# Decode attention on one core: GpSimd hands VectorE its first credits, and ends only after the last wide value matmuls

## The chip, the cores and the metric

One core of a Trainium2 chip. The metric is the device time of one execution in microseconds (us). Every run whose state the record gives is fast, with a mean granted clock of 0.799 to 0.818. "Span" is the time from the first to the last instruction of the program in the profile; the metric is 1.7 to 1.8 us longer than the span in most profiled executions.

A few words on names. The kernel programs the engines by hand. In its code an engine waits for a semaphore to reach a number, or takes (waits and subtracts); another engine or a load adds. A "credit" is such an addition given ahead of time, so that the first pass through a loop does not wait for something that has not happened yet. PE is the TensorE, DVE the VectorE, ACT the ScalarE, POOL the GpSimd, SP the SyncE.

## The reference

Attention for one query token: 32 query heads, 8 key/value heads, 65,536 keys, head size 128, bfloat16.

```python
B, Hq, Hkv, Sq, Sk, D = 1, 32, 8, 1, 65536, 128
k = jnp.repeat(k, Hq // Hkv, axis=1); v = jnp.repeat(v, Hq // Hkv, axis=1)
scores = jnp.einsum("bhqd,bhkd->bhqk", q, k) * D ** -0.5
return jnp.einsum("bhqk,bhkd->bhqd", softmax(scores, axis=-1), v)
```

Keys and values together are 268 MB, each byte used once. The arithmetic per byte is small.

## The kernel before

There are eight groups (one key/value head each), and each has two key blocks and two value blocks of 128 x 256 rows. SyncE issues all loads; VectorE transposes keys and weights; TensorE makes scores and the weighted sum of values; ScalarE does the exponential; GpSimd only clears buffers, copies 16 columns of the query per group, and gives credits. These are the parts that matter here (cuts marked `# ...`):

```python
# SyncE
load_k(0, 0)
load_k(0, 1)
sp.sem_inc(s_vd, 2)                 # VectorE's two credits for its value weights
for g in range(1, G):
    for b in range(2):
        load_k(g, b)                # waits for score matmuls (s_sc)
        load_v(g - 1, b)            # waits for value matmuls (s_vc), then gives s_vd
# ...
# GpSimd, start
GP.mark(gp.memset(wz[:, :, :], 0.0))
gp.memset(zs[:, :], 0.0).then_inc(s_cl, 1)    # credit: the sum buffer is clear
n = GP.mark(gp.memset(ident[:, :], 0.0))
# ... identity matrix
gp.sem_inc(s_v[1], 16 * (2 * G - 3))
gp.sem_inc(s_v[2], 16)
# ...
# VectorE, one group (loop)
y_sum()                             # takes s_cl
transposes(0, 0, SL)                # keys, first block
# ...
transposes(1, 0, 128)
d_take(s_vd)
weights(1)                          # writes the buffer that the value matmuls read
transposes(1, 128, SL)
# ...
# GpSimd, end
GP.wait((s_sc, 16 * G))
gp.sem_inc(s_sd, 1)
GP.wait((s_dv, d_sum(G)))
gp.sem_inc(s_w, 4)
```

The last value block is loaded in eight pieces. The first three (records 101 to 103 in the trace's own numbering) feed the "wide" matmuls; the last five are small and feed 32 small matmuls, then ScalarE scales the result and stores 1 KB.

Of the kernel before, what the change touches and what calls it, by code (L numbers as in the profile page):

```python
# [19 lines left out]
G = 8  # L20
# [29 lines left out]
def kernel(  # L50
# [15 lines left out]
    def sb(name, shape, dt):  # L66
        return ctx.enter_context(nc.sbuf_tensor(name, shape, dt))
# [4 lines left out]
    def sem(name):  # L72
        return ctx.enter_context(nc.semaphore(name))
# [17 lines left out]
    zs = sb("zs", [P, 1024 + 4 * D + D + 2], fp32)  # L91
# [21 lines left out]
    s_sc, s_pe, s_vb, s_vc = sem("s_sc"), sem("s_pe"), sem("s_vb"), sem("s_vc")  # L113

    s_sd, s_vd, s_pt, s_ex, s_ds = sem("s_sd"), sem("s_vd"), sem("s_pt"), sem("s_ex"), sem("s_ds")
    s_cl, s_ga = sem("s_cl"), sem("s_ga")
# [11 lines left out]
    sp, act, dve, gp, pe = nc.sync, nc.scalar, nc.vector, nc.gpsimd, nc.tensor  # L128
# [3 lines left out]
    GP = Queue(nc, gp, s_gp)  # L132
# [16 lines left out]
    def load_k(g, b):  # L149
        SP.wait((s_sc, 16 * g - 8 + 8 * b if g else 0))  # L150
        cuts = k_lo + [SL] if (g, b) in ((0, 0), (G - 1, 1)) else [0, 128, SL] if g == 0 else [0, SL]
        for lo, hi in zip(cuts, cuts[1:]):
            load(k, g, b, 1 + b, s_k[b, lo], lo, hi)
# [23 lines left out]

    load_k(0, 0)
    load_k(0, 1)

    sp.sem_inc(s_vd, 2)
    for g in range(1, G):
        for b in range(2):
            load_k(g, b)
# [5 lines left out]
    act.dma_start(out=q_in[:, :], in_=q[0, :, 0, :]).then_inc(s_q, 16)  # L190

    GP.mark(gp.memset(wz[:, :, :], 0.0))
    gp.memset(zs[:, :], 0.0).then_inc(s_cl, 1)
    n = GP.mark(gp.memset(ident[:, :], 0.0))
    GP.after(n)
    p_ident = GP.mark(gp.affine_select(
        out=ident[:, :], in_=ident[:, :], compare_op=ALU.not_equal, fill=1.0, base=0,
        pattern=[[-1, P]], channel_multiplier=1,
    ))

    gp.sem_inc(s_v[1], 16 * (2 * G - 3))

# [22 lines left out]
    def d_sum(g):  # L225
        return d_qT + 4 * g + 1
# [296 lines left out]
    gp.sem_inc(s_sd, 1)  # L523
    GP.wait((s_dv, d_sum(G)))
    gp.sem_inc(s_w, 4)


# [28 lines left out]
```

## Time and profile before

| | before |
|---|---|
| time, median of the first 3 runs | 629.46 us (629.42 to 630.25) |
| span of the profiled run | 627.8 us |
| load queue, share of the 16 DMA engines' span | 99.1% |
| moved | 268.45 MB at 428 GB/s |
| PE / DVE / ACT / POOL busy | 56% / 55% / 5% / 1% |

First, the page of the kernel before: busy time with its share of the span and number of instructions, then the DMA queues with packets, MB, and share.

```profile
span 627.8 us, 7062 instructions
PE 354.6 (56%) x2142; PEld 139.1 (22%) x2142; DVE 345.5 (55%) x154; ACT 34.4 (5%) x26; POOL 8.8 (1%) x40
...
q1 hardware_dynamic: 6944, 268.45, 99.1%
q8 instruction: 1, 0.02, 0.0%
q10 hardware_dynamic: 56, 0.01, 0.0%
q14 instruction: 1, 0.01, 0.0%
```

No engine is near 100% except the DMA engines (99.1%): the kernel is bound by its loads. The two queues that the profile marks `instruction` and not as data (q8 and q14): each holds one packet within the span, of 16,384 and 8,192 bytes.

The table of windows of the kernel before: window, length, busy us of each engine with counts, granted TensorE clock, DMA share, GB/s.

```profile
core 0: us, PE busy (x) PEld busy (x) DVE busy (x) ACT busy (x) POOL busy (x), PEclk, DMA share, GB/s
40.00:80.00 40.00, 24.40 (x93) 9.49 (x92) 30.76 (x15) 3.94 (x3) 0.77 (x4) 0.80 1.00 433
...
610.00:622.00 12.00, 7.24 (x61) 2.15 (x62) 0.60 (x1) 0.00 (x0) 0.00 (x0) 0.59 0.98 407
622.00:628.00 6.00, 2.48 (x40) 2.01 (x34) 1.47 (x4) 0.36 (x1) 0.00 (x0) 0.97 0.20 67
```

Loads fill everything but the last few us (DMA share 0.98 from 610 to 622 us, 0.20 after). What the last few us hold is shown by the end of the chain of waits (start, length, what):

```profile
608.60 12.41 DMA io<-in_v_dram
621.00 0.04 issue
621.05 1.02 PE acc L253 x5
622.07 0.02 PE pb L347
622.10 1.84 PE pf L358 x28
623.94 0.32 PE pf L247 x2
624.26 0.24 PE pf L358 x4
...
624.59 0.36 ACT o L486
```

The store that follows is issued at 624.98 us and lands at 626.36 us; then comes a closing barrier to 627.8 us. GpSimd leads that barrier: the last of the others comes at 626.74 us, GpSimd's wait is at 626.77, its release at 627.21, and the waits of the four others follow at 627.25 to 627.26 us. Its instructions there, by the view of the program's closing line (count, shortest/median/longest ns, first and last start):

```profile
L551 POOLq EVENT_SEMAPHORE  x4: 17/17/17, 626.8 to 627.7; - x4
L551 POOLq DRAIN  x3: 34/34/112, 612.0 to 627.5; - x3
```

The four semaphore instructions are wait, release, wait, release. The trace has them at 626.77, 627.21, 627.62 and 627.70 us: 0.44 us from the first wait to its release, but 0.08 us for the second pair.

### The profile page before, as it was taken

The page shows a single profiled execution, that of the slowest core. Times are in us where ns is not written, and L with a number is a line of the kernel's source. Part 1 is how long each engine was busy: PE and PEld are TensorE (multiplying, and loading weights), DVE is VectorE, ACT ScalarE, POOL GpSimd, SP SyncE. Part 2 cuts the span into 40 slices and gives each one's busy share as a digit, 9 for nine tenths or more (in the row PEclk, how much of TensorE's full clock was granted, in tenths as well). Part 3 has the DMA queues.
Part 4 walks back from the last instruction along what each step waited for, and adds up shares of the span by engine and source line. Part 5 has one row for each costly group of instructions (what it writes and reads, how often), then busy time and mean ns, then how long its engine had stood idle before and what let it go on. Part 6 is the DMA issues. An engine that isn't in the chain of part 4 may idle for free. (4 is left out here: it accounts for less than half of the span.)

```text
span 627.8 us, 7062 instructions
## 1 busy us (share of the span) xinstructions
PE 354.6 (56%) x2142; PEld 139.1 (22%) x2142; DVE 345.5 (55%) x154; ACT 34.4 (5%) x26; POOL 8.8 (1%) x40
## 2 busy tenths in 40 slices
PE   1865483827638275481844808458183571886346
PEld 0322131312213032130321303123031230332112
DVE  7795835649066490754807557084670946684210
ACT  0000100020000200002000020000200002000100
POOL 2000000000000000000000000000000000000000
PEclk9979596977959679596785968859588695899676
DMA  8999999999999999999999999999999999999996
GB/s 366 436 468 401 468 401 468 401 468 401 468 401 468 401 468 401 468 401 459 409 455 413 443 426 434 434 422 447 413 455 409 459 401 468 401 434 434 434 434 269
DMA packets 7002, 268.48 MB, mean 428 GB/s; under 512 B 856, under 2 KB 1112, under 8 KB 1496
## 3 DMA queue, kind: packets, MB, share of 16 engines
q1 hardware_dynamic: 6944, 268.45, 99.1%
q8 instruction: 1, 0.02, 0.0%
q10 hardware_dynamic: 56, 0.01, 0.0%
q14 instruction: 1, 0.01, 0.0%
HBM read 268.44 MB, written 0.01 MB: 428 GB/s over the span
## 5 line engine op out<-in xcount | busy, mean ns | idle before, releaser
L300 PE MATMUL acc<-io,wz 128*128 x1024 | 271.0, 417 | 187.2 <-PEq L121 157.5
L372 DVE STREAM_TRANSPOSE io<-io 128x4096 uint32<-128x4096 uint32 x64 | 279.9, 4416 | 157.9 <-DVEq L121 157.9
L300 PEld LDWEIGHTS acc<-io,wz 128*128 x1024 | 105.8, 103 | 352.4 <-issue 273.6
L253 PE MATMUL acc<-io,et 128*16 128x512 bf16 x1016 | 72.4, 416 | 19.3 <-PEq L121 19.2
L439 ACT ACTIVATE zs<-acc,nmb 128x2048 bf16<-128x2048 f32 x8 | 15.7, 1967 | 556.5 <-DVE nmb L419 556.5
L409 DVE TENSOR_REDUCE mg<-acc 128x1 f32<-128x2048 f32 x8 | 18.3, 2292 | 48.2 <-DVEq L121 48.2
L253 PEld LDWEIGHTS acc<-io,et 128*16 128x16 bf16 x1016 | 27.6, 94 | 58.5 <-issue 35.6
L247 PE MATMUL pf<-zs,sel 128*4 128x130 f32 (+1 forms) x20 | 5.7, 387 | 53.3 <-PEq L121 53.3
L375 DVE STREAM_TRANSPOSE et<-zs 128x1024 bf16<-128x1024 bf16 x17 | 20.8, 1226 | 22.7 <-SPq L158 12.8
L449 ACT ACTIVATE acc<-wz 128x2560 f32<-128x2560 bf16 (+2 forms) x8 | 16.3, 2040 | 1.0 <-ACT zs L439 0.2
L411 DVE TENSOR_REDUCE m<-pt 1x4 f32<-1x128 f32 x8 | 2.2, 279 | 22.6 <-DVEq L121 22.6
L518 POOL COPY wz<-qT 32x16 bf16<-32x16 bf16 x32 | 6.1, 192 | 513.3 <-PE acc L300 441.1
L325 PE MATMUL pt<-et 128*16 128x512 bf16 x32 | 13.1, 411 | 0.0
L247 PEld LDWEIGHTS pf<-zs,sel 128*4 128x4 f32 x20 | 1.1, 83 | 53.9 <-issue 53.7
L383 DVE TENSOR_REDUCE zs<-zs 128x128 f32<-128x512 f32 x9 | 6.1, 681 | 7.6 <-DVEq L121 7.6
L422 DVE TENSOR_TENSOR zs<-acc,sely 128x512 f32<-128x512 f32 x8 | 8.5, 1064 | 0.0
L471 DVE TENSOR_TENSOR zs<-acc,sely 128x512 f32<-128x512 f32 x1 | 0.7, 691 | 11.5 <-PE acc L253 11.5
L342 PE MATMUL pb<-ident,nrow 1*128 1x1 f32 x8 | 1.5, 189 | 7.5 <-PEq L121 7.5
L325 PEld LDWEIGHTS pt<-et 128*16 128x16 bf16 x32 | 3.1, 97 | 4.5 <-issue 1.4
L340 PE MATMUL pt<-ident,mg 128*1 128x128 f32 x8 | 2.2, 270 | 2.6 <-PEq L121 2.6
L419 DVE COPY nmb<-pb 128x1 f32<-128x1 f32 x8 | 1.3, 159 | 3.9 <-DVEq L121 3.9
L204 DVE MEMSET acc<- 128x2560 f32 x1 | 2.2, 2192 | 1.6 <-SPq L64 1.6
(29 smaller groups left out, 20.6 us busy)
## 6 DMA issues: line engine op xcount, KB each, us to landing
io<-in_v_dram SPq DMA_DIRECT2D x5, 4096.0 KB, 17.0
io<-in_k_dram SPq DMA_DIRECT2D x8, 2048.0 KB, 27.3
io<-in_k_dram SPq DMA_DIRECT2D x2, 4096.0 KB, 34.2
io<-in_v_dram SPq DMA_DIRECT2D x1, 2048.0 KB, 10.3
io<-in_v_dram SPq DMA_DIRECT2D x1, 1024.0 KB, 12.4
io<-in_v_dram SPq DMA_DIRECT2D x3, 256.0 KB, 12.8
io<-in_v_dram SPq DMA_DIRECT2D x2, 128.0 KB, 12.9
io<-in_k_dram SPq DMA_DIRECT2D x13, 48.4
```

Source lines behind the costliest of these rows:

```text
L247: return pe.matmul(out=pf[0:H, 0:w], lhsT=sel[:, :], rhs=vs[:, 0:w], skip_group_check=True, **kw)
L253: return pe.matmul(out=vacc[32 * c:32 * c + 16, :, :], lhsT=et[:, ch // 2, w0:w0 + 16], rhs=io[:, PS * ch + 4 * tt:PS * ch + 4 * tt + 4, : ...
L300: i = pe.matmul(out=bass.AP(acc, r_o, [[2560, P], [1, 512]]), lhsT=bass.AP(wz, r_w + ((2 * s + e) * WB - 4 * u), [[4 * WB, P], [1, P]]), r ...
L325: pe.matmul(out=pt[0:16, :], lhsT=et[:, 0, 0:16], rhs=et[:, 0, :], start=True, stop=True)
L372: dve.transpose(out=part, in_=part).then_inc(s_kt, 2)
L375: dve.transpose(out=et[:, :, :].rearrange("p i n -> p (i n)"), in_=ex[:, 2 * b:2 * b + 2, :].rearrange("p i n -> p (i n)"),).then_inc(s_et, 1)
L383: DV.mark(dve.tensor_reduce(out=vs[:, 0:D], in_=vy[:, :, :], axis=AX.X, op=ALU.add))
L409: dve.tensor_reduce(out=mg[:, :], in_=sc, axis=AX.X, op=ALU.max).then_inc(s_mg, 1)
L422: dve.tensor_tensor(out=vy[:, :, :].rearrange("p d y -> p y d"), in0=vacc, in1=sely[:, :, None].to_broadcast([P, 4, D]), op=ALU.mult,).the ...
L439: act.activation(out=ex[:, :, :].rearrange("p b n -> p (b n)"), in_=sc, func=ACT.Exp, bias=nmb[:, :], scale=SCALE, accum_out=vs[:, D + g % ...
L449: act.activation(out=part, in_=wz[:, 0, 0:1].to_broadcast([P, part.shape[1]]), func=ACT.Copy).then_inc(s_cl, 1)
L518: gp.tensor_copy(out=wz[r, :, c0:c0 + H].rearrange("p (s w) h -> p s w h", s=2), in_=qTb[r, :, :, g, :],).then_inc(s_w, 1)
```

## The change

The stated intent: GpSimd shall end only after the last wide value matmuls, and shall give VectorE its first credits in SyncE's place. It has three instructions more; SyncE one less.

```diff
     load_k(0, 0)
     load_k(0, 1)
-
-    sp.sem_inc(s_vd, 2)
     for g in range(1, G):
@@
     GP.mark(gp.memset(wz[:, :, :], 0.0))
-    gp.memset(zs[:, :], 0.0).then_inc(s_cl, 1)
+    GP.mark(gp.memset(zs[:, :], 0.0))
     n = GP.mark(gp.memset(ident[:, :], 0.0))
@@
+    gp.sem_inc(s_vd, 2)
+    gp.sem_inc(s_cl, 1)
 
     gp.sem_inc(s_v[1], 16 * (2 * G - 3))
@@
     GP.wait((s_dv, d_sum(G)))
     gp.sem_inc(s_w, 4)
+    GP.wait((s_vb, 2 * G))
```

## The prediction

> **What bounds the kernel.** The loads. The table of DMA queues gives the load queue 99.1% of the 16 engines' span: 268.45 MB at 428 GB/s in 627.8 us. No compute engine is near that (PE 56%, DVE 55%, POOL 1%; first part of the page). In the table of windows the DMA share is 0.97 to 1.02 in every stretch from 40 to 610 us. Only the ends are not load time: the first load is issued at 0.96 us; after the last value bytes (about 623.8 us) come the last small matmuls (to 624.5), the scaling on ScalarE (0.36 us), the 1 KB store (issued 624.98, landed about 626.4) and the closing barrier (to 627.8).
>
> **What the change does, with costs.**
> 1. SyncE loses one semaphore instruction (17 ns in the records) at 4.07 us, behind the six first key loads. It then waits tens of us for score matmuls before its next load. Worth: 0.
> 2. GpSimd gives VectorE's two credits instead, and the clearing credit becomes an instruction of its own, no longer tied to the end of the 1.49 us clearing of the zeros tile. Both fall at about 3.4 us, beside the identity's last step (3.40 us, 0.29 us); the two increments already there are recorded at 3.36 and 3.44 us, so two more are an estimated 0.1 us. VectorE takes the clearing credit near 4.8 us, but its sum starts at 5.56 us behind four transposes, and it then waits until 8.4 us for keys anyway. The other credit is first taken at about 41 us. GpSimd's next copy has 1.9 us of slack. Worth: 0.
> 3. GpSimd's last wait. Before, GpSimd's last useful step is at 594.24 us, SyncE holds it until 611.9 us, and it sits in the closing barrier until 626.77. Now it leaves at about 622.1 us, still 4.5 us ahead of the store's landing that the barrier waits for. Worth: 0 on the chain of waits.
> 4. Side effect: instruction fetch. [...] one 16,384-byte packet on an instruction queue at 623.23 us, taking 1.09 us, right as the loads end. If it is GpSimd's, it can move by some us; before the last value bytes it could delay one DMA engine by up to 1.1 us. And between GpSimd's wait and its release in the closing barrier lie 0.44 us at 626.77, against 0.08 us at the two other such places; if that is a fetch, three more instructions may move it out of the chain (-0.36 us), or not.
>
> **Sum.** 0 on the load stream, -0.4 to +1.1 us at the end, most likely near 0. Runs of the kernel before already spread from 629.42 to 630.25.
>
> Predicted 629.4 us; 8 in 10 between 628.5 and 630.4. Chances: faster by over 2% 0.01, within 2% 0.98, slower by over 2% 0.01.
>
> **What would show it.** Load queue again 99%, about 428 GB/s; first key transpose at about 8.4 us; first value weights at about 41.5 us; GpSimd's final drain at about 622.1 us instead of 612.0; the last chain (value load, small matmuls, scaling, store) the same within 0.3 us. The 16 KiB packet's time and the 0.44 us pause tell step 4.
>
> **What would make it wrong.** A hidden dependence on when GpSimd idles or fetches (a fetch that stalls a DMA engine for longer than its packet's 1.1 us), credits later than VectorE needs them, so that the first group's order shifts and later loads with it[...].

The sum came to -0.4 us (0.44 less 0.08 us) to +1.1 us (the 1.09 us of the one packet on q8), both estimates from the trace of the kernel before.

## The result

Ratios here are the mean time of one kernel's fast runs over that of the other's of the same rounds, so not quite the ratio of the medians quoted.

The changed kernel takes 629.38 us (median of 6 runs, 629.05 to 629.69), the kernel before 629.44 us (median of 6, 629.27 to 630.25). The ratio is 0.9997, 95% interval 0.9984 to 1.001: the same. A second comparison of five rounds (below) gave 0.9994, 0.998 to 1.0007. The timings alone do not resolve a gain.

The profile after, in the same order as before:

```profile
span 627.3 us, 7064 instructions
PE 354.5 (57%) x2142; PEld 139.3 (22%) x2142; DVE 345.5 (55%) x154; ACT 34.4 (5%) x26; POOL 8.8 (1%) x40
...
q1 hardware_dynamic: 6944, 268.45, 99.2%
q8 instruction: 1, 0.02, 0.0%
q10 hardware_dynamic: 56, 0.01, 0.0%
q14 instruction: 2, 0.02, 0.0%
```

The loads are as before. One line differs: queue 14 has two instruction packets within the span instead of one. The trace has the extra one, 8,192 bytes, at 623.53 us, taking 0.31 us; in the kernel before one of the same size came at 627.90 us, just after the span.

The end of the chain of waits after the change:

```profile
608.69 12.42 DMA io<-in_v_dram
621.11 0.04 issue
621.15 1.02 PE acc L254 x5
622.17 0.02 PE pb L348
622.20 1.90 PE pf L359 x28
624.09 0.22 PE pf L248 x2
624.31 0.24 PE pf L359 x4
...
624.64 0.36 ACT o L487
```

Up to ScalarE's last step the two kernels agree within 0.15 us at each piece (624.59 and 624.64 us at the end). The span is 0.45 us shorter nevertheless, so the difference lies behind it, in the closing barrier:

```profile
L553 POOLq EVENT_SEMAPHORE  x4: 17/17/17, 626.7 to 627.2; - x4
L553 POOLq DRAIN  x3: 34/34/64, 622.8 to 627.1; - x3
```

GpSimd's first wait is at 626.73 us (626.77 before), its release at 626.81 us (627.21 before): the pause went from 0.44 to 0.08 us, and that 0.36 us is most of the 0.45 (0.04 us lie before the first wait, and the longest drain behind the release is 0.05 us shorter, 64 ns after 112). It did not vanish, it moved: GpSimd's new last wait is at 622.23 us, and the next instruction, a drain, only at 622.65 us, 0.42 us later (0.14 us for the same pair in e1_wait_only below), where nobody waits for GpSimd.

The credits did nothing to the start. VectorE's first instructions on keys and its first value weights, from the timelines of the kernel before and of the kernel after:

```profile
8.39 4.45 DVE L372 STREAM_TRANSPOSE io<-io 128x4096 uint32<-128x4096 uint32 x1 [2.15 <-DVEq L121]
...
41.50 1.20 DVE L375 STREAM_TRANSPOSE et<-zs 128x1024 bf16<-128x1024 bf16 x1
```

```profile
8.40 4.45 DVE L373 STREAM_TRANSPOSE io<-io 128x4096 uint32<-128x4096 uint32 x1 [2.17 <-DVEq L121]
...
41.50 1.20 DVE L376 STREAM_TRANSPOSE et<-zs 128x1024 bf16<-128x1024 bf16 x1
```

### The profile page after: what moved, and what is told of

It is laid out like the page before. It is cut to its first block, busy times and chain, and to the rows that moved or that the text cites. A ratio compares the mean times of both kernels' runs of the same rounds, so it can differ in the third digit from the quotient of the medians.

```text
span 627.3 us, 7064 instructions
## 1 busy us (share of the span) xinstructions
PE 354.5 (57%) x2142; PEld 139.3 (22%) x2142; DVE 345.5 (55%) x154; ACT 34.4 (5%) x26; POOL 8.8 (1%) x40
## 3 DMA queue, kind: packets, MB, share of 16 engines
q1 hardware_dynamic: 6944, 268.45, 99.2%
```

## The experiments

Two theories of the pause. **Leave-time**: the pause is what GpSimd pays for having sat in the barrier from 612 us on; leaving at 622 us cures it. **Instruction-place**: the pause lies at one fixed place in GpSimd's stream of instructions, and a packet that the profile marks as instructions goes with it (after the change, 8,192 bytes at 623.53 us, 1.3 us behind GpSimd's last wait). Where that place falls is a matter of counting instructions. Below, this place is called the crossing and the packet GpSimd's fetch; what GpSimd does at the place was not shown. A third, **chance**, says that it comes and goes. The twelve runs below all gave correct results, and all had five rounds.

### e1_wait_only: the last wait alone (one instruction more)

```diff
     gp.sem_inc(s_w, 4)
+    GP.wait((s_vb, 2 * G))
```

> Only the last wait of the change (GpSimd also waits for the last wide value matmuls); the credits stay as before. All theories: time within 0.2% of before, because the load queue (99% of the span) is untouched. The pause of 0.44 us between GpSimd's wait and its release in the closing barrier tells them apart. Leave-time theory: the pause is a price for having sat in the closing barrier since 612 us, so it falls to about 0.08 us and the span by about 0.36 us. Instruction-place theory: [...] this adds one of the change's three, so it need not fall. Chance theory: it comes and goes in any kernel.

Measured: 629.05 us (628.80 to 629.33), ratio 0.9991 (0.9977 to 1.0004). Pause 0.085 us; GpSimd's packet at 623.81 us. Span 627.48 us. Both theories are still possible, as the kernel leaves later and has another instruction.

### e2_credits_only: the credits alone (two instructions more)

The diff of the change without its last line.

> Only the credits' move to GpSimd (two more instructions there, one less on SyncE), without the last wait. All theories: time within 0.2% of before; first key transpose on VectorE at 8.4 us, first value weights at 41.5 us. Leave-time theory: GpSimd's last drain is at 612 us again and the pause stays at 0.44 us. Instruction-place theory: the pause may fall to 0.08 us, as GpSimd's later instructions stand two places further on.

Measured: 630.22 us (629.35 to 630.35), ratio 1.0003 (0.999 to 1.0017). GpSimd stops at 612 us as before, yet the pause is 0.083 us: the leave-time theory is in trouble. GpSimd's two drains, 0.10 us apart before, are 0.47 us apart here (611.94 and 612.40 us): the pause is there now. And the packet is fetched at 616.07 us, in the middle of the last value loads. The landing records of those loads show what that does. Record 103 has 16 reports, read here as one from each of the 16 DMA engines; the last three reports of record 101 (the load in flight before the fetch) and of 103 (after it) are, in us:

| | 101, last three | 103, last three |
|---|---|---|
| before | 613.58, 613.58, 613.62 | 620.98, 620.98, 621.00 |
| e2_credits_only | 613.60, 613.61, 613.70 | 621.00, 621.11, 621.53 |

One engine falls 0.42 us behind the next, in a load for which the wide matmuls wait. This was not expected.

There is a second thing in this trace. Its chain of waits has 2.74 us for the 28 small matmuls that took 1.84 us before:

```profile
622.62 2.74 PE pf L359 x28
```

The windows of this kernel around it (the clock is the third figure from the right):

```profile
618.10:621.50 3.40, 1.24 (x17) 0.44 (x17) 0.00 (x0) 0.00 (x0) 0.00 (x0) 1.00 0.99 398
621.50:624.90 3.40, 3.33 (x34) 2.75 (x35) 1.47 (x4) 0.00 (x0) 0.00 (x0) 0.50 0.52 177
624.90:628.40 3.50, 0.90 (x13) 0.67 (x11) 0.00 (x0) 0.36 (x1) 0.00 (x0) 0.99 0.01 3
```

The granted clock was 0.50 for exactly the 3.4 us in which the small matmuls ran, so they took 0.9 us longer. In the other 13 traces the clock was full from 622.7 us at the latest. The clock records of the kernels before and after have stretches at 0.5 or 1.0 of 3.41, 6.83, 10.24 us and so on; what sets them was not shown. Two of the five executions of this kernel had spans of 627.6 and 627.7 us. So this 0.9 us belongs to the execution, not to the credits.

### e3_pad3: three idle instructions more, nothing else

```diff
+    for _ in range(3):
+        gp.sem_inc(s_pad, 1)        # a semaphore that nobody reads
     gp.sem_inc(s_v[1], 16 * (2 * G - 3))
```

> The kernel before with three increments of an unused semaphore on GpSimd at the place where the change puts its credits: nothing but three instructions more. Time within 0.2% of before. Leave-time theory: pause 0.44 us, last drain at 612 us. Instruction-place theory: pause 0.08 us, span 0.36 us shorter, as after the change, which also adds three.

Measured: 630.34 us (629.35 to 630.74), ratio 1.0013 (0.9999 to 1.0026). Pause 0.079 us with the last drain at 612 us: the instruction-place theory's figure. But the span of the profiled run is 627.61 us, not 0.36 us shorter: the packet comes at 598.47 us, and the slowest DMA engine is 0.58 us behind the next in record 103. What the pause gave back, the lag took: the last store went out at 625.37 us, 0.40 to 0.54 us later than in the two traces of the kernel before.

### e4_before_again: the kernel before as a null run

> The kernel before, unchanged, as a null run: ratio 1.000 within 0.1%. Its trace shows whether the 0.44 us pause and the span of 627.8 us repeat. Leave-time and instruction-place theories: pause 0.44 us again. Chance theory: the pause may be 0.08 us.

Measured: 629.39 us (629.24 to 629.58), ratio 0.9998 (0.9984 to 1.0011). Pause 0.440 us again; lag 0.03 us. Chance is now unlikely, and the fourteen traces together leave it no room. The span was 627.45 us against 627.80 us in the first trace of the same kernel, so one span is no measure of 0.36 us (0.21 us of this difference is the last store's own time, 1.17 against 1.38 us); the pause and the lag, read as differences inside one trace, are.

### e5_pad1: one idle instruction more

The edit of e3_pad3 with a range of 1.

> The kernel before with one increment of an unused semaphore more on GpSimd at the start, no last wait. Instruction-place theory (the first four experiments gave it): [...] it pauses for about 0.36 us and soon after an 8,192-byte instruction packet is fetched. One instruction more puts the crossing between GpSimd's drain at 612.0 us and its wait in the closing barrier. So: pause in the closing barrier 0.08 us; an 8,192-byte packet at about 616 us; the last DMA engine's share of the final value loads 0.4 to 0.55 us behind the next one's, last value bytes at about 624.2 us instead of 623.8. Net on the span about +0.05 us (+0.4 lag, -0.36 pause), if the clock in the tail is full. Leave-time theory: GpSimd leaves at 612 us as before, so pause 0.44 us, no packet before 624 us, no lag.

Measured: 629.49 us (629.40 to 631.07), ratio 1.0006 (0.9992 to 1.002). Pause 0.086 us, packet at 615.91 us, lag 0.37 us, span 627.66 us, last value bytes at 624.04 us. The place was foretold from counting alone. The leave-time theory falls here: this kernel leaves GpSimd idle from 612 us as before and does not pause.

### e6_pad20: twenty idle instructions more

> Twenty increments more instead of one. Instruction-place theory: the crossing falls behind the last copy for the fourth group, at about 291 us, and the packet is fetched at about 295 us, in the middle of the load stream. If a lag of one DMA engine is kept until the end, the slowest engine is 0.4 to 0.55 us behind the next in the last value loads, as with a fetch at 598 us; if it is made up in 320 us of loading, the gap is below 0.1 us as in the kernel before and the span about 0.36 us shorter than before. Time within 0.2% of before either way.

Measured: 629.37 us (629.25 to 629.53), ratio 0.9997 (0.9984 to 1.0011). Pause 0.078 us; lag 0.46 us at the end. In this trace the last report of each earlier load was at most 0.04 us behind the one before it up to 274.6 us, and 0.48 us in the next load, at 294.4 us: an engine that fell behind in mid-kernel did not catch up in the 340 us of loading that were left. The packet came at 283.63 us and not at 295 as expected. Why it came 7 us before the copy at 290.8 us, behind which it was expected, was not shown.

### e7_six_fewer: six instructions fewer

Six semaphore increments of GpSimd are given by ScalarE instead (two after its first load, two after the scores of the first key block, two after those of the second).

> Six semaphore increments of GpSimd are moved to ScalarE (credits that are first needed much later), no last wait, so GpSimd leaves at 612 us. Instruction-place theory: the crossing falls six instructions later, just behind the last one of the span: pause 0.08 us, no 8,192-byte packet of GpSimd's before 627 us, no lag of a DMA engine (gap below 0.1 us), span about 0.36 us shorter than before: 627.1 to 627.5 us, time about 629.1 us at full clock in the tail. Leave-time theory: pause 0.44 us, span as before.

Measured: 629.72 us (629.32 to 629.77), ratio 1.0001 (0.9987 to 1.0014). Pause 0.079 us, no packet of GpSimd's before 627 us, lag 0.08 us, span 627.49 us: all as expected, but the time was to be 629.1 us and is 629.72. This is the one profiled run in which time minus span is not 1.7 to 1.8 us: it is 2.23 us. It is no single look: the five executions of this kernel have 2.17 to 2.23 us, and the 88 executions of the other kernels and of the kernel before whose spans were recorded with the experiments have 1.68 to 1.88 us. So a pause's worth has left the span, not the time: it seems to lie in the 2.17 to 2.23 us that the metric has beyond the span (the pause is not itself in the trace).

### e8_two_fetches: two crossings within the loads

131 idle increments on GpSimd after its copies for the second group.

> 131 increments of an unused semaphore on GpSimd after its copies for the second group, where it idles (67 to 125 us). [...] GpSimd crosses twice within the loads: among these increments at about 70 us, and, 128 instructions on, behind its step at 594.5 us as with three increments. Instruction-place theory: two 8,192-byte packets, at about 70 to 75 us and at about 598 us; if both fall on the same DMA engine, its lag doubles to about 0.8 to 1.1 us in the last value loads and the span grows by about 0.5 us more; if on two engines, two engines lag by 0.4 to 0.55 us and the span is as with one fetch. Leave-time theory: no lag, pause 0.44 us.

Measured: 629.97 us (629.88 to 630.24), ratio 1.0007 (0.9994 to 1.0021). The page of this kernel shows three packets on queue 14:

```profile
span 628.1 us, 7193 instructions
...
q14 instruction: 3, 0.02, 0.0%
```

They are at 73.09, 599.02 and 625.56 us (the last is another engine's: every trace has one near the last store). Inside the row of idle increments, otherwise 0.08 us apart, there is one step of 0.43 us, at 69.45 us. Counted over GpSimd's recorded instructions, the step at 594.5 us, behind which the second crossing was expected, is the 128th after this one (before the run, 128 was an assumption). After two fetches one DMA engine alone is 1.00 us behind the next in record 103 (622.10 against 621.10 us). The loads of this trace show it in two steps: at most 0.03 us up to 61.8 us, 0.31 to 0.36 us from 81.5 to 594.6 us, 0.92 to 1.02 us from 605.0 us on. This is the dose-response: no fetch in the loads 0.02 to 0.09 us, one 0.32 to 0.58, two 1.00.

### e9_wait_same_count: the last wait, at an unchanged count

```diff
     gp.sem_inc(s_v[1], 16 * (2 * G - 3))
-    gp.sem_inc(s_v[2], 16)          # given by ScalarE instead
@@
     gp.sem_inc(s_w, 4)
+    GP.wait((s_vb, 2 * G))
```

> The change's last wait alone, but with one increment of GpSimd's moved to ScalarE, so that GpSimd has as many instructions as in the kernel before. GpSimd leaves at about 622.2 us. Instruction-place theory: the crossing stays where it was before, between GpSimd's wait and its release in the closing barrier: pause 0.44 us, no 8,192-byte packet of GpSimd's before 627 us, span 627.5 to 627.8 us. Leave-time theory: pause 0.08 us, as with the wait alone.

Measured: 629.47 us (629.44 to 629.88), ratio 0.9995 (0.9981 to 1.0009). GpSimd leaves at 622.1 us, and the pause is 0.439 us:

```profile
L551 POOLq EVENT_SEMAPHORE  x4: 17/17/17, 626.7 to 627.6; - x4
L551 POOLq DRAIN  x3: 34/34/112, 622.2 to 627.4; - x3
```

With e5_pad1 this completes the square: late leaving without another instruction leaves the pause, another instruction without late leaving removes it.

### e10_after_again: the change again

> The change as it is, five times beside the kernel before on one chip. Instruction-place theory: pause 0.08 us, the packet at about 623.5 us, gap of the slowest DMA engine in the last wide value load below 0.1 us; where the granted clock in the last 3 us is full, span about 627.1 to 627.5 us, 0.3 to 0.4 us below the kernel before with the same clock; ratio 0.999 to 1.000.

Measured: 629.17 us (629.00 to 630.13), ratio 0.9994 (0.998 to 1.0007). Pause 0.078 us, packet at 623.25 us, lag 0.04 us in record 103, span 627.32 us. Only the very last small load (record 108) has an engine 0.28 us late.

### e11_late_credit: credits that are really late

```diff
-    sp.sem_inc(s_vd, 2)
@@
                 for t in k_lo[1::2]:
                     gp.sem_inc(s_k[0, t], 16 * (2 * G - 2))
+                GP.wait((s_sc, 12))
+                gp.sem_inc(s_vd, 2)
```

(and one other increment moved to ScalarE, to keep the count).

> The two credits of VectorE are given by GpSimd only after the score matmuls of the first half of the second key block (about 43 us), the number of GpSimd's instructions unchanged. This is a real lateness, against none in the change: first value weights at 43 to 44 us instead of 41.5, the next key transpose 1.5 to 2.5 us later. Load-bound theory: the loads in flight cover it, so the time is within 0.1% of before and the last value load is issued within 0.5 us of 608.2 us. Rival (credits are on the critical path): the time grows by 1.5 to 2.5 us.

Measured: 632.93 us (632.21 to 633.20), ratio 1.0047 (1.0033 to 1.006): slower by about 3 us, more than either theory said (it is under 2%, but the interval excludes no change). The credit came at 47.8 us, not at 43, so VectorE stood still for 6.50 us, as its timeline shows:

```profile
47.98 1.25 DVE L372 STREAM_TRANSPOSE et<-zs 128x1024 bf16<-128x1024 bf16 x1 [6.50 <-DVEq L121]
```

SyncE's next key load went out at 63.65 us instead of 57.23, and the value load of 94.89 us at 101.36. By then the queue had run low. The windows of 96 to 104 us, in the kernel before and in this one:

```profile
96.00:104.00 8.00, 0.00 (x0) 0.00 (x0) 3.44 (x1) 0.00 (x0) 0.00 (x0) 0.76 0.91 393
```

```profile
96.00:104.00 8.00, 5.22 (x72) 2.06 (x70) 3.54 (x1) 0.00 (x0) 0.00 (x0) 1.00 0.69 262
```

From the load of 167.78 us (171.09 here) every load up to the first piece of the last value block is 3.2 to 3.7 us late, and the pieces after it 2.8 us. Of 6.45 us of lateness about 3.1 us were covered by the loads in flight (6.45 less 3.3; an estimate). So the load-bound theory as I put it was wrong: the first group's credits do reach the load stream. In the change they are given at about 3.4 us and used at 41.5 us, which is why they cost nothing.

### e12_wait_last: GpSimd waits for the very last matmul

```diff
-    GP.wait((s_vb, 2 * G))
+    GP.wait((s_pe, 1))
```

(on the changed kernel).

> As after the change, but GpSimd waits for the very last matmul instead of the last wide one, so its crossing, pause and fetch fall at about 624.5 to 625.5 us, behind all value loads and before the store's landing. Instruction-place theory: pause in the closing barrier 0.08 us, packet at about 625.2 us, span equal to that after the change or up to 0.1 us shorter (the packet at 623.5 us still met the last bytes). If the packet meets the store's descriptors instead, the span could be up to 0.3 us longer.

Measured: 629.61 us (629.49 to 630.60), ratio 1.0001 (0.9987 to 1.0015). Pause 0.079 us, but the last store took 1.75 us from issue to landing, 1.16 to 1.49 us in the other traces, and the span was 627.76 us. GpSimd's packet is one of two, at 624.57 and 625.57 us, one of which falls within the store's flight. In the other traces the other engine's packet starts between 0.72 us before and 0.02 us after the store's issue (624.98 us here), so the one at 625.57 us is GpSimd's. It ended at 625.94 us, 0.95 us after the issue, and the store's last 256-byte packet started just then, against 0.81 to 0.82 us after the issue elsewhere. So the fetch seems to have held up the store, and the order of all fourteen stores (below) supports it; no run was made to test this. Later is not better than the change's place.

### All traces together

Lag is the last report of record 103 less the one before it. "Fetch" is GpSimd's own packet, told by its moving with the crossing.

| kernel | GpSimd's instructions | leaves at us | pause us | fetch at us | lag us | span us |
|---|---|---|---|---|---|---|
| before / again | 0 | 612 | 0.44 / 0.44 | 627.9 / 627.7 | 0.02 / 0.03 | 627.80 / 627.45 |
| e9_wait_same_count | 0 | 622 | 0.44 | 628.0 | 0.09 | 627.69 |
| e5_pad1 | +1 | 612 | 0.09 | 615.9 | 0.37 | 627.66 |
| e2_credits_only | +2 | 612 | 0.08 | 616.1 | 0.42 | 628.50 (half clock) |
| e3_pad3 | +3 | 612 | 0.08 | 598.5 | 0.58 | 627.61 |
| e6_pad20 | +20 | 612 | 0.08 | 283.6 | 0.46 | 627.60 |
| e8_two_fetches | +131 | 613 | 0.08 | 73.1, 599.0 | 1.00 | 628.14 |
| e7_six_fewer | -6 | 612 | 0.08 (time minus span is longer by about 0.45) | behind the span | 0.08 | 627.49 |
| e11_late_credit | 0 | 615 | 0.44 | 631.0 | 0.03 | 630.94 |
| e12_wait_last | +3 | 625 | 0.08 | 625.6 | 0.06 | 627.76 |
| e1_wait_only | +1 | 622 | 0.09 | 623.8 | 0.03 | 627.48 |
| the change / again | +3 | 622 | 0.08 / 0.08 | 623.5 / 623.2 | 0.07 / 0.04 | 627.35 / 627.32 |

A count confirms the instruction-place theory: in each trace in which the pause can be seen, it lies between GpSimd's 68th and 69th recorded instruction, wherever that falls (the barrier in before, e4, e9 and e11; the new last wait in the change and e12; the drains in e2; the idle increments in e8). Where that place is at 612.0 us or earlier, in the full load stream, GpSimd's packet starts 3.6 to 4.5 us behind it (e6 aside, where the packet came before the step behind which it was expected); where it is at 621.7 us or later, 1.0 to 1.5 us behind it. (e7 is left out: its packet is one of two behind the span.) So the pause of 0.36 us does not wait for this packet to land.

Each span can be cut at the last store's issue and landing. From the landing to the end it is 1.44 us in the four traces with the pause in the barrier and 1.03 to 1.09 us in the ten others. This is the gain of the change, clear of the scatter. The store's own time follows the fetches near it: in eight traces the other engine's packet was over by 0.2 us after the store's issue, and the store took 1.16 to 1.17 us; in five (the first trace before and the first after among them) the packet lasted to 0.34 to 0.55 us after the issue, and the store took 1.29 to 1.49 us; in e12 GpSimd's lasted to 0.95 us, and the store took 1.75 us.

With the store's time above 1.16 us taken out, the spans with neither pause nor lag in them (e1, e7, e12, the change twice) are 627.16 to 627.32 us, those with the pause (before, e4, e9) 627.44 to 627.69 us, and those with one lag at full clock (e3, e5, e6) 627.46 to 627.61 us. The mean difference is about 0.35 us, or 0.06% of the time. Five rounds of timing, with intervals of about 0.13% to either side, do not resolve it.

No version here beats the change by more than the spread. e1_wait_only, one line, does the same.

## Why the prediction was right

- **The load stream untouched (steps 1 and 2): right.** Load queue 99.2% after 99.1%, 428 GB/s in both, first key transpose at 8.40 us, first value weights at 41.50 us. But e11 shows that this rested on the credits being early, not on their being harmless: the prediction named their lateness among what could make it wrong, and weights that came 6.5 us later made the loads 3.3 us late and the time about 3 us longer.
- **GpSimd's later end off the chain (step 3): right.** Its final drain is at 622.8 us, not 622.1, as the crossing's pause sits before it; still 3.9 us ahead of the barrier's first wait.
- **Instruction fetch (step 4): the right suspect and the right size of the gain, but offered only as a possibility; wrong in the packet and in the size of the risk.** The pause fell by the 0.36 us that was named ("or not"), because the instructions added moved it; one would have done (e1, e5). The 16,384-byte packet is not GpSimd's: it stays between 622.8 and 623.9 us in all but the late-credit kernel, where it moves with the end (626.6). GpSimd's is one of 8,192 bytes that lay just behind the span. And the cost of a fetch among the loads was put at up to 1.1 us; measured, one fetch left its DMA engine 0.32 to 0.58 us behind.
- **The sum: right.** -0.4 to +1.1 us at the end, most likely near 0; the two pairs of traces give -0.45 and -0.13 us in the span (0.35 us of scatter lies between the two traces before alone), and the times are 629.44 and 629.38 us. That the median lies within 0.02 us of the predicted 629.4 us is luck: the six runs spread over 0.64 us.
- **The chance of a faster or slower result over 2%: rightly small.** Nothing touched here is worth more than 1 us of 629.

What stays open: some executions are near 630.2 us while most are near 629.4 (among them one of the change's second five, four of e3's five, five of the nine of the kernel before beside e9 to e12), and one of e5's is at 631.07 us. The half clock of e2's trace gives a cause of the right size (0.9 us), but none of the other long executions was traced, so for those it is only argued. Also open is why the crossing itself costs 0.36 us: no DMA packet that could be GpSimd's falls into it.

## What to carry to other kernels

When a kernel is bound by loads, count what each engine does late: here a single 8,192-byte instruction fetch among the loads (load queue 99.1% busy) put one of 16 DMA engines 0.32 to 0.58 us behind, which was still there 340 us later (e6), and with it the last value bytes came at 624.04 us instead of 623.84 (e5). Here a wait that parked a nearly idle engine until the wide value loads were over moved both its pause (to 622.2 us) and its fetch (to 623.5 us) to where nobody waited, but it was the place in the instruction stream that decided (e5, e9), so test such a change with idle instructions before crediting the edit. And before calling a credit free, delay it on purpose: here it had 38 us in hand, but when VectorE got it 6.5 us too late, the kernel took about 3 us longer.
